# Attention and token mixer on one core: a written order of steps replaced by another

## The chip, the core and the metric

The kernel runs on one core of a Trainium2 chip. The metric is the device time of one execution in microseconds (us), the median over runs. The engines are named as in the profile: PE is TensorE's products, PEld its weight loads, DVE is VectorE, ACT is ScalarE, POOL is GpSimd and SP is SyncE, which here only issues DMAs.

## The reference

There are 8 batches of 8 heads, 576 tokens and 64 values per head, and 32 packed queries p.

```python
def sm_attn(qq, kk, vv):
    s = scale * np.matmul(qq, kk.transpose(0, 1, 3, 2))
    a = np.exp(s - np.max(s, axis=-1, keepdims=True))
    a = a / (np.sum(a, axis=-1, keepdims=True) + 1e-09)
    return np.matmul(a, vv)

p_packed = sm_attn(p, k, v)
x = sm_attn(q, p_packed, p_packed)          # heads side by side: (8, 576, 512)
wq, wk = x @ w_q, x @ w_k                   # (512, 64) each
W_tok = scale * np.einsum('bsd,btd->bst', wq, wk)
mixed = np.einsum('bst,btd->bsd', W_tok, x)
out = np.maximum(mixed, 0.0) @ w_out        # (512, 512), float32
```

## The kernel before

The work is cut into steps with short names, and a string named `ORDER` (lines 13 to 57) lists them one after the other. A loop at the end of the kernel (lines 602 to 624) reads a step such as `AM.3.2@P` or `OT.2.0=2,3`: the name, the batch, mostly a part of the batch, after `@` the engine (A ScalarE, V VectorE, P GpSimd, S SyncE) and after `=` the banks of the accumulator memory (PSUM, 8 banks) that its result takes. Under `tc.manual_schedule()` each engine runs its own steps strictly in that order; across engines they wait by semaphores for data, and for a buffer or a bank to come free.

For one batch the steps are these. KT (a block transpose of k on VectorE, line 237, as are TE, PT and QV), S1 (scores of p and k, line 282), X1 (exponential, two halves, ScalarE, line 293), TE (transposes of the exponentials), PV (their product with v and a column of ones, line 315), RC and PP (one over the sum, and the packed values, lines 319 and 323), PT (their transpose, `ppT`). QK multiplies ppT with w_q and w_k (line 336), QKE copies it out and QD doubles a part of it on GpSimd. QV transposes q, S2 multiplies it with ppT (line 373; parts 0 and 1 are two tiles of 128 tokens each, 2 is the rest, 3 is four tiles at once), X2 is its exponential (line 378), RS and RR its sums and their reciprocals (lines 394 and 399), and AM the product `a` = exponential times reciprocal (line 405), on GpSimd or VectorE. AT transposes a on TensorE (lines 414 and 419), AE copies that out, WKQ makes wk and wq (lines 441 and 446) and WE copies them out. The token mixing is regrouped: GM is a^T wk (line 467), Y is that times the packed values (line 477), MX and MR are mixed's columns (lines 492 and 498), with the copies GE and YE between them. RL, RLF (quarter of a relu) and RLR are the relus (line 503 on ScalarE, 505 on VectorE), OT and OH the product with w_out (lines 540 and 580), and OE, OEF and OEH copy it out of the accumulator memory (lines 128 and 132), from which ST, STF and STH store it. OT.b.4 is the last ninth of the tokens of a pair of batches.

Loads (LD, lines 157 to 182) are issued on GpSimd's own queue, since they turn float32 into bf16 on the way. A GpSimd load has one of eight semaphores in turn, so it is issued only when the eighth before it has landed, and what stands behind it on GpSimd waits too. k, q and v have four buffers each, results for storing six (`o`), the exponentials and most others two or three. HOLD.v7 is a tiny DMA on SyncE's queue that waits for the last v, so that the stores queued behind it on that engine start only then.

WARM steps are products of zeros that go nowhere, in float32, in pieces of at most 512 columns (the number is in units of 128 columns); they fill stretches in which TensorE has to wait. They are on line 619.

```python
                n = 128 * int(f[1])
                wide = int(f[2]) if len(f) > 2 else 512
                while n > 0:
                    w = min(n, wide)
                    ...
                    nc.tensor.matmul(bank(int(bk), [w]), warm[:, 0:P], rhs, start=True, stop=True)
                    n -= w
```

## Time and profile before

| | |
|---|---|
| median of 3 runs | 104.53 us (104.41 to 104.62) |
| profiled execution, first to last instruction (span) | 102.8 us, granted clock 1.000 |
| profiled execution's own time | not given apart; the median of the runs is 1.73 us above the span |
| TensorE, VectorE, ScalarE, GpSimd busy | 92.7, 73.7, 65.0, 51.8 us |
| read and written in device memory | 30.15 MB and 9.44 MB |

The rows of a timeline show the start in us, the duration in us, the engine, the line, the operation, the tile written and the tile read with their shapes, and how many instructions were put together; in brackets stands how long the engine sat idle before it and whose work ended that. Groups show the sum of busy time in us, the mean duration of one in ns and, behind the bar, the idle time before them. Ends of TensorE's products are modelled, so two rows can overlap by some tenths.

### The profile page before, as it was taken

How to read it: one execution, taken by the hardware profiler on the slowest of the kernel's cores; microseconds unless marked ns; L12 is line 12 of the kernel's file. 1: busy time of each engine (PE TensorE's matmuls, PEld its weight loads, DVE VectorE, ACT ScalarE, POOL GpSimd, SP SyncE). 2: the span in 40 equal slices, each digit the busy share in tenths (PEclk: the TensorE clock that was granted, in tenths of full speed). 3: DMA queues.
4: the chain of work that ended last, by engine and by line, in shares of the span. 5: the costliest groups of instructions: out<-in, count | busy, mean ns of one | idle time of the engine just before them, and what ended most of it. 6: DMA issues, size and time to landing. Idle time of an engine off the chain costs nothing.

```text
span 102.8 us, 3593 instructions
## 1 busy us (share of the span) xinstructions
PE 92.7 (90%) x1536; PEld 54.6 (53%) x1536; DVE 73.7 (72%) x140; ACT 65.0 (63%) x111; POOL 51.8 (50%) x81
## 2 busy tenths in 40 slices
PE   5995999998698899999998899989999999999940
PEld 3894454555364733655546556643757664743420
DVE  4173366966979479898597979689999979339520
ACT  2320406168853767938986979897889897735540
POOL 5971866993029938925349574558615009100000
PEclk9999999999999999999999999999999999999999
DMA  0999999999999999999999999999999999986894
GB/s 9 249 230 207 213 210 213 207 209 213 205 211 207 212 211 210 213 205 212 211 212 207 211 213 204 217 211 203 255 262 409 411 410 408 418 345 264 335 364 160
DMA packets 13279, 25.13 MB, mean 244 GB/s; under 512 B 1040, under 2 KB 6416, under 8 KB 13008
## 3 DMA queue, kind: packets, MB, share of 16 engines
q0 software_dynamic: 9648, 17.04, 84.0%
q1 hardware_dynamic: 3056, 7.41, 19.0%
q10 hardware_dynamic: 560, 0.46, 1.7%
q8 instruction: 12, 0.20, 0.7%
q14 instruction: 3, 0.02, 0.1%
HBM read 30.15 MB, written 9.44 MB: 385 GB/s over the span
## 4 chain that ended last, share of the span: by engine, by line
PE 49%; DMA 21%; DVE 8%; POOL 7%; ACT 6%; issue 3%; SPq 1%; DVEq 0%; POOLq 0%; ACTq 0%
PE ps L540 26%; DMA q_sb<-in_q_dram 13%; DMA o<-in_moe_w_q_dram 8%; PE ps L373 4%; POOL a L405 4%; PE ps L315 3%; ACT e1T L293 3%; PE ps L419 3%; PE ps L446 3%; DVE rs L394 2%; PE ps L441 2%; PE ps L467 2%; PE ps L282 2%; ACT e L378 1%; DVE qT L237 1%
## 5 line engine op out<-in xcount | busy, mean ns | idle before, releaser
L540 PE MATMUL ps<-wout,relu 128*128 128x512 bf16 x124 | 30.6, 380 | 0.0
L405 POOL TENSOR_TENSOR a<-e,rr 128x256 bf16<-128x256 f32 (+2 forms) x18 | 19.5, 1099 | 17.9 <-DVE rr L399 7.0
L619 PE MATMUL ps<-o 128*128 128x128 f32 (+3 forms) x76 | 19.5, 401 | 1.2 <-DVE o L135 1.2
L540 PEld LDWEIGHTS <-relu 128*128 128x128 bf16 x124 | 10.7, 98 | 11.7 <-issue 1.1
L128 ACT ACTIVATE o<-ps 128x1024 f32<-128x1024 f32 (+2 forms) x13 | 11.3, 871 | 5.4 <-PE ps L540 5.2
L619 PEld LDWEIGHTS ps<-o 128*128 128x128 f32 x76 | 11.3, 209 | 5.2 <-issue 3.6
L503 ACT ACTIVATE relu<-ps 128x1024 bf16<-128x1024 f32 (+1 forms) x14 | 13.0, 968 | 1.1 <-PE ps L492 1.1
L293 ACT ACTIVATE e1T<-ps 128x576 bf16<-128x576 f32 x16 | 9.8, 656 | 5.8 <-PE ps L282 5.2
L378 ACT ACTIVATE e<-ps 128x256 f32<-128x256 f32 (+2 forms) x19 | 11.2, 623 | 2.7 <-PE ps L373 2.5
L394 DVE TENSOR_REDUCE rs<-e 128x16 f32<-128x512 f32 (+2 forms) x13 | 10.9, 840 | 2.3 <-ACT e L378 2.2
L237 DVE STREAM_TRANSPOSE kT<-k_sb 128x1152 uint32<-128x1152 uint32 (+1 forms) x9 | 11.1, 1230 | 1.9 <-DMA k_sb<-in_k_dram 1.9
L173 POOL DMA_DIRECT2D v_sb<-in_v_dram x16 | 10.0, 628 | 4.0 <-DMA v_sb<-in_v_dram 1.6
L237 DVE STREAM_TRANSPOSE qT<-q_sb 128x1152 uint32<-128x1152 uint32 (+1 forms) x10 | 11.0, 1108 | 0.1
L132 DVE COPY o<-ps 128x1024 f32<-128x1024 f32 (+2 forms) x7 | 6.8, 977 | 5.3 <-PE ps L540 2.7
L237 DVE STREAM_TRANSPOSE e<-e1T 128x288 uint32<-128x288 uint32 x16 | 7.4, 468 | 3.1 <-ACT e1T L293 2.7
L128 ACT ACTIVATE aT<-ps 128x128 bf16<-128x128 f32 (+2 forms) x11 | 5.0, 465 | 5.7 <-PE ps L419 3.3
L128 ACT ACTIVATE wkq<-ps 128x448 bf16<-128x448 f32 (+1 forms) x10 | 7.2, 730 | 1.8 <-PE ps L446 1.7
L315 PE MATMUL ps<-v_sb,e 64*64 64x192 bf16 x288 | 7.5, 245 | 0.8 <-DVE e L237 0.5
L315 PEld LDWEIGHTS <-e 64*64 64x64 bf16 x288 | 5.9, 107 | 2.6 <-DVE e L237 2.1
L373 PEld LDWEIGHTS <-qT 64*128 64x128 bf16 x320 | 5.4, 94 | 2.8 <-DVE qT L237 1.7
L373 PE MATMUL ps<-ppT,qT 64*128 64x64 bf16 x320 | 6.6, 190 | 0.2 <-DVE qT L237 0.2
L446 PE MATMUL ps<-aT,pqk 128*128 128x256 bf16 (+1 forms) x48 | 6.8, 246 | 0.0
(70 smaller groups left out, 130.3 us busy)
## 6 DMA issues: line engine op xcount, KB each, us to landing
v_sb<-in_v_dram POOLq DMA_DIRECT2D x16, 288.0 KB, 13.9
out_dram<-o SPq DMA_DIRECT2D x9, 512.0 KB, 9.3
k_sb<-in_k_dram POOLq DMA_DIRECT2D x7, 576.0 KB, 13.6
q_sb<-in_q_dram POOLq DMA_DIRECT2D x6, 576.0 KB, 13.6
out_dram<-o POOLq DMA_DIRECT2D x2, 1024.0 KB, 11.3
out_dram<-o SPq DMA_DIRECT2D x5, 256.0 KB, 2.5
q_sb<-in_q_dram POOLq DMA_DIRECT2D x4, 288.0 KB, 10.4
out_dram<-orem SPq DMA_DIRECT2D x3, 256.0 KB, 8.5
```

What stands on the lines that cost most here:

```text
L128: nc.scalar.activation(o, i, COPY)
L173: nc.gpsimd.dma_start(v_bufs[b % NL][halves(i), 0:7:2], src)
L237: nc.vector.transpose(o, i)
L293: nc.scalar.activation(e1T[:, x], T["s1", b][x].rearrange("a c m -> a m c"), EXP, scale=scale)
L315: nc.tensor.matmul(T["pv", b][halves(cc), i], lhsT, rhs, start=n == 0, stop=n == R - 1, skip_group_check=True)
L373: nc.tensor.matmul(ps[:, y, t - t0, i], lhsT, rhs, start=e == 0, stop=e == 1)
L378: nc.scalar.activation(e2[:, t0:t1].rearrange("a t (i y n) -> a y (t i) n", i=2, y=2), T["s2", b, c].rearrange("a y t i n -> a y (t i) n") ...
L394: nc.vector.tensor_reduce(rs[:, t0 * H:t1 * H], src, axis=AX, op=ADD)
L405: e.tensor_tensor(a2[:, t0:t1].rearrange("a t i (u l) -> a (t i u) l", l=L), e2v(b, c), T["rr", b][:, t0 * H:t1 * H].to_broadcast((P, (t1 ...
L503: nc.scalar.activation(o, i, RELU)
L540: nc.tensor.matmul(ps, lhsT, wout[:, j, :], start=j == 0, stop=j == NJ - 1)
L619: nc.tensor.matmul(bank(int(bk), [w]), warm[:, 0:P], rhs, start=True, stop=True)
```

## The change

Only the string `ORDER` is another one. It has two lines fewer, so that every later line of the kernel has a number smaller by 2. Up to the transposes of batch 0 (`AT.0.1`) each engine keeps its order, with other banks; from there on the steps of all batches stand in another order. Two fillers of three units are added (behind `AT.0.1` there are six runs where there were four), and others moved. Some steps go to another engine: the products AM.1.1, AM.3.2, AM.4.2, AM.6.2 and AM.7.0 from GpSimd to VectorE and AM.6.3 back, YE.0 and YE.3 to ScalarE, YE.2, YE.5 and YE.7 to VectorE, QKE.1, QKE.3 and QKE.5 to ScalarE and QKE.4 to VectorE, and some copies and relus. The load of v7 is issued behind the two halves of q7 (r7 and q7), where it stood ahead of them, and the three stores that GpSimd issues are moved behind all loads.

```diff
-S1.1=0,1,4,5 WE.0.1@A GM.0=6 X1.1.0@A TE.1.0@V GE.0@A WARM.2=7 Y.0=2,3 YE.0@V S1.2=0,1,6,7 MR.0=2,3 X1.1.1@A
-TE.1.1@V MX.0.0=4,5 X1.2.0@A LD.O PV.1.0=0,1 TE.2.0@V PV.1.1 X1.2.1@A TE.2.1@V RC.1@V LD.k3 PP.1.0@V PP.1.1@V
-PT.1@V MX.0.1=6,7 QV.1.2@V RLR.0@A QK.1=2 QKE.1@V RL.0.0@A WARM.3=3 S2.1.2=4,5 S2.1.0=0,1 RL.0.1@A X2.1.2@A
-RS.1.2@V RR.1.2@V S2.1.1=2,3 X2.1.0@A RS.1.0@V RR.1.0@V WARM.1=6 PV.2.0=6,7 PV.2.1 X2.1.1@A RS.1.1@V RC.2@V
...
-HOLD.v7 MR.3=0,1 RC.5@V PP.5.1@V OE.2.1@A MX.3.0=2,3 PP.5.0@V PT.5@V MX.3.1=6,7 RLR.3@A RL.3.0@A OT.3.4=0
...
-STF.6.3 YE.7@A ST.5.0 MR.7=6,7 RLR.7@A MX.7.0=4,5 RLF.7.0.1@A RLF.7.0.0@V MX.7.1=2,3 RLF.7.1.0@A OT.7.4=0
-OEF.7.4@A ST.7.4 RLF.7.1.1@V OT.7.1=6 OEF.7.1@V OT.7.0=7 STF.7.1 OT.7.2=1 OEF.7.0@A OH.7.0=0 STF.7.0 OEF.7.2@A
...
+AT.0.1=1 AE.0.1@A AE.0.0@V WKQ.0.0=6,7 WKQ.0.2 WE.0.0@A LD.q2 WKQ.0.1 KT.2.2@V S1.1=2,3,4,5 WE.0.1@A WARM.3=0
+X1.1.1@A TE.1.1@V LD.O GM.0=0 X1.1.0@A GE.0@A S1.2=6,7,4,5 Y.0=2,3 TE.1.0@V X1.2.1@A PV.1.0=0,1 PV.1.1 X1.2.0@A
+YE.0@A TE.2.0@V MX.0.1=4,5 RC.1@V WARM.3=6 WARM.2=6 PP.1.1@V MX.0.0=6,7 PP.1.0@V WARM.3=2 PT.1@V QK.1=0 RL.0.0@A
+QV.1.2@V TE.2.1@V S2.1.2=2,3 QKE.1@A S2.1.0=6,7 X2.1.2@A LD.k3 MR.0=0,1 RS.1.2@V X2.1.0@A WARM.1=2 S2.1.1=2,3
...
+RS.3.4@V RR.3.4@V RL.2.1@A RC.4@V OT.2.0=4,5 PP.4.1@V LD.v6 AM.3.2@V OT.2.1 AM.3.3@P QD.3@P PP.4.0@V AT.3.2=0
...
+WKQ.3.1 X2.4.2@A WE.3.2@A KT.5.2@V OT.2.2=0,1 RS.4.4@V S1.5=2,3,6,7 RR.4.4@V OT.2.3 AM.4.3@P LD.q6 X1.5.1@A
+MR.2=4,5 GM.3=6 QK.4=7 X1.5.0@A OE.2.1@A TE.5.1@V TE.5.0@V GE.3@A PV.5.0=2,3 Y.3=0,1 LD.k7 RLR.2@V AM.4.2@V QKE.4@V
...
+WE.7.0@A GM.7=2 GE.7@A OE.5.0@V ST.4.0 ST.2.1 OT.6.1 OE.6.0@A Y.7=4,5 YE.7@V OT.6.2=2,3 MX.7.1=0,1 MX.7.0=4,5
+ST.1.8@P ST.5.1 ST.5.0 MR.7=6,7 RLF.7.0.0@V OEF.6.2@A RLF.7.0.1@A OT.6.3 RLF.7.1.1@V STF.6.2 ST.6.0 RLF.7.1.0@A
+RLR.7@V OT.7.0=4 OT.7.1=5 OEF.7.1@A OEF.6.3@V OEF.7.0@V STF.6.3 OT.7.2=0 OT.7.4=1 OH.7.0=2 OEF.7.2@V OH.7.1=0
```

TensorE around the end of PV.1 and QK.1 (the rows of lines 492 and 490 are MX.0, 336 and 334 QK.1, 619 and 617 fillers, 373 is S2.1), before:

```order
L336 LDWEIGHTS ppT_1_250
L336 MATMUL ps_61<-wqk_63,ppT_1_250 64x128
L619 MATMUL ps_61<-o_1_86 128x384
L373 LDWEIGHTS qT_1_268
L373 MATMUL ps_61<-ppT_1_250,qT_1_268 128x64
```

and now:

```order
L490 LDWEIGHTS y_0_502
L490 MATMUL ps_61<-wkq_0_363,y_0_502 128x512
L617 MATMUL ps_61<-o_1_86 128x384
L617 MATMUL ps_61<-o_1_86 128x256
L490 LDWEIGHTS y_0_502
L490 MATMUL ps_61<-wkq_0_363,y_0_502 128x512
L490 LDWEIGHTS y_0_502
L490 MATMUL ps_61<-wkq_0_363,y_0_502 128x512
L617 MATMUL ps_61<-o_1_86 128x384
L334 LDWEIGHTS ppT_1_250
L334 MATMUL ps_61<-wqk_63,ppT_1_250 64x128
```

The filler of 384 columns has moved from behind QK.1 to ahead of it, and two more runs stand between the halves of MX.0.

ScalarE over the same stretch (e1T is X1, g GE, rem RLR, relu RL, e2 X2, y YE, pqk QKE), before:

```order
L293 ACTIVATE e1T_0_194<-ps_61 128x576
L128 ACTIVATE g_0_420<-ps_61 128x128
L293 ACTIVATE e1T_0_194<-ps_61 128x576 x3
L503 ACTIVATE rem_0_522<-ps_61 128x4x64
L503 ACTIVATE relu_0_534<-ps_61 128x1024 x2
L378 ACTIVATE e2_1_84<-ps_61 128x2x2x64
L378 ACTIVATE e2_1_84<-ps_61 128x2x4x64 x2
```

and now:

```order
L291 ACTIVATE e1T_0_194<-ps_61 128x576 x2
L126 ACTIVATE g_0_423<-ps_61 128x128
L291 ACTIVATE e1T_0_194<-ps_61 128x576 x2
L482 ACTIVATE y_0_502<-ps_61 128x256
L501 ACTIVATE relu_0_526<-ps_61 128x1024
L126 ACTIVATE pqk_1_264<-ps_61 128x2x128
L376 ACTIVATE e2_1_84<-ps_61 128x2x2x64
L376 ACTIVATE e2_1_84<-ps_61 128x2x4x64 x2
L501 ACTIVATE relu_0_526<-ps_61 128x1024
L501 ACTIVATE rem_0_629<-ps_61 128x4x64
```

YE.0 and QKE.1 have come to ScalarE, and RL.0.1 and RLR.0 have moved behind X2.1.

VectorE from batch 3's sums to the start of batch 5 (rs is RS, rr RR, rec RC, pp PP, qT QV, ppT PT, aT AE, kT KT, e1 TE), before:

```order
L394 TENSOR_REDUCE rs_0_283<-e2_1_84 128x40
L399 RECIPROCAL rr_1_286<-rs_0_283 128x40
L319 RECIPROCAL rec_1_240<-ps_61 128x2
L323 SCALAR_TENSOR_TENSOR pp_1_244<-ps_61,rec_1_240,mask_79 128x128 x2
L237 STREAM_TRANSPOSE ppT_1_250<-pp_1_244 128x128
L237 STREAM_TRANSPOSE qT_1_268<-q_sb0_73 128x2x2x288
L132 COPY aT0_80<-ps_61 128x2x512
L237 STREAM_TRANSPOSE kT_1_124<-k_sb1_70 128x2x2x288
L394 TENSOR_REDUCE rs_0_283<-e2_0_83 128x40
L399 RECIPROCAL rr_0_285<-rs_0_283 128x40
L237 STREAM_TRANSPOSE e1_1_197<-e1T_0_194 128x9x32 x2
L486 TENSOR_SCALAR y_0_429<-ps_61 128x256
```

and now:

```order
L392 TENSOR_REDUCE rs_0_283<-e2_1_84 128x40
L397 RECIPROCAL rr_1_286<-rs_0_283 128x40
L317 RECIPROCAL rec_1_240<-ps_61 128x2
L321 SCALAR_TENSOR_TENSOR pp_1_244<-ps_61,rec_1_240,mask_79 128x128
L403 TENSOR_TENSOR a2_0_328<-e2_1_84,rr_1_286 128x256
L321 SCALAR_TENSOR_TENSOR pp_1_244<-ps_61,rec_1_240,mask_79 128x128
L235 STREAM_TRANSPOSE qT_1_268<-q_sb0_73 128x2x2x288
L235 STREAM_TRANSPOSE ppT_1_250<-pp_1_244 128x128
L130 COPY aT0_80<-ps_61 128x2x512
L235 STREAM_TRANSPOSE kT_1_124<-k_sb1_70 128x2x2x288
L392 TENSOR_REDUCE rs_0_283<-e2_0_83 128x40
L397 RECIPROCAL rr_0_285<-rs_0_283 128x40
```

AM.3.2 (the row of line 403) has come in between the two halves of PP.4, and PT.4 stands behind QV.4; behind these rows VectorE does TE.5, RLR.2, AM.4.2 and QKE.4 ahead of RC.5, where before it did TE.5 and YE.3.

## The prediction

> **What bounds the kernel now.** I read the totals first, then busy time by stage, then TensorE's own rows in each stage with the waits in brackets, and last what VectorE, ScalarE and GpSimd do at those waits. The totals:

> ```profile
> span 102.8 us, 3593 instructions
> ...
> PE 92.7 (90%) x1536; PEld 54.6 (53%) x1536; DVE 73.7 (72%) x140; ACT 65.0 (63%) x111; POOL 51.8 (50%) x81
> ...
> HBM read 30.15 MB, written 9.44 MB: 385 GB/s over the span
> ```

> TensorE is busy for 90% of the span, and no other engine comes near. The stages (start:end, length, then busy us and count for TensorE, its weight loads, VectorE, ScalarE and GpSimd, then granted clock, DMA share, GB/s):

> ```profile
> 36.00:51.10 15.10, 14.91 (x250) 7.45 (x245) 12.13 (x20) 11.39 (x18) 8.36 (x12) 1.00 1.15 210
> 51.10:68.60 17.50, 16.18 (x354) 9.64 (x352) 14.54 (x26) 15.26 (x24) 11.33 (x14) 1.00 1.14 210
> 68.60:79.20 10.60, 10.60 (x198) 6.35 (x202) 10.36 (x16) 8.93 (x15) 5.54 (x6) 1.00 1.13 274
> 79.20:99.00 19.80, 19.67 (x243) 10.73 (x242) 13.34 (x26) 13.58 (x26) 2.86 (x4) 1.00 0.93 369
> ```

> From 36.0 to 99.0 us TensorE idles 0.19 + 1.32 + 0.00 + 0.13 = 1.64 us. That, and what stands before 36.0, is all that another order can win, since the products after that point are the same ones. The only stage with something to lose from is 51.1 to 68.6, where VectorE and ScalarE are at 83% and 87%. The clock is 1.00 throughout. The last stage has a second limit: the DMA share is 0.93, so a faster TensorE there gains at most 0.07 x 19.8 = 1.4 us before the stores bound it.

> **The change, part by part.** No work is added but fillers; steps change place and engine. The queues of waiting work on VectorE, ScalarE and GpSimd decide, so I walk TensorE through the new order with durations of before.

> *The front (first difference at 22 us).* ScalarE and TensorE in before:

> ```profile
> 24.58 1.19 ACT L293 ACTIVATE e1T<-ps 128x576 bf16<-128x576 f32 x2 [0.27 <-PE ps L282]
> 25.66 0.39 ACT L503 ACTIVATE rem<-ps 128x256 bf16<-128x256 f32 x1
> 25.92 1.96 ACT L503 ACTIVATE relu<-ps 128x1024 bf16<-128x1024 f32 x2
> 29.28 1.36 ACT L378 ACTIVATE e<-ps 128x256 f32<-128x256 f32 x3 [1.40 <-PE ps L373]
> ```
> ```profile
> 27.51 0.41 PE L336 MATMUL ps<-wqk,ppT 64*64 64x128 bf16 x8 [0.97 <-DVE ppT L237]
> 27.85 0.91 PE L619 MATMUL ps<-o 128*128 128x384 f32 x2
> 28.94 0.78 PE L373 MATMUL ps<-ppT,qT 64*128 64x64 bf16 x40 [0.18 <-DVE qT L237]
> ```
> ```profile
> 31.24 1.32 PE L619 MATMUL ps<-o 128*128 128x512 f32 x4
> 32.44 0.40 PE L419 MATMUL ps<-idb,a 128*128 128x128 bf16 x4
> ```

> The filler of 640 columns took from 31.24 to 32.44, 0.24 us per 128 columns. Two more runs of 384 columns are 6 x 0.24 = 1.44 us of TensorE. They are not all lost: they stand where QK.1 waited 0.97 us at 27.51. YE.0 goes from VectorE to ScalarE, behind X1.2's two exponentials, which end at 25.77; with 0.3 for itself MX.0.1 starts at about 26.05. Then come half an MX, 640 columns of filler, the other half, 384 columns: 26.05 + 0.3 + 1.2 + 0.3 + 0.7 = 28.6 for QK.1 (27.51 before). But the filler that stood behind QK.1 now stands ahead of it, so S2.1.2 follows at about 29.1 against 28.94. Between S2.1.0 and S2.1.1 the 128-column filler now writes S2.1.2's bank and so waits for X2.1.2, which has QKE.1 ahead of it on ScalarE: S2.1.1's exponential ends at about 31.4, not 29.28 + 1.36 = 30.64.

> ```profile
> 31.34 2.05 POOL L405 TENSOR_TENSOR a<-e,rr 128x512 bf16<-128x512 f32 x2 [0.22 <-DVE rr L399]
> ```
> ```profile
> L237 DVE STREAM_TRANSPOSE qT<-q_sb 128x1152 uint32<-128x1152 uint32 x6 | 8.1, 1350 | 0.1
> ```
> ```profile
> 34.97 0.78 PE L373 MATMUL ps<-ppT,qT 64*128 64x64 bf16 x40
> 35.68 0.47 PE L467 MATMUL ps<-wkq,a 128*128 128x64 bf16 x10
> 35.98 0.38 PE L540 MATMUL ps<-wout,relu 128*128 128x512 bf16 x1
> ```

> AM.1.1 was the second half of GpSimd's 2.05 us and ended at 33.39. On VectorE it is shorter, which gives back most of the 0.76: it ends at about 33.5. QV.2.2, of 1.35 us, is queued behind it and PT.2, so it ends at 35.1, S2.2.2 starts at 35.15 (34.97), and WE.1.1, now on VectorE behind QV.2.2, holds GM.1 to 35.9. The first output product starts at 36.3 instead of 35.98: **+0.3**. If a producer's end and its reader's start never overlap as they do in these rows, the same walk gives +1.2; if the fillers fall wholly into waits, 0. I take +0.3, since pairs such as the 1.19 and 1.96 above show overlap.

> *36 to 51 us.* 0.19 us of idle in 15.1 and neither VectorE (12.1) nor ScalarE (11.4) is short; PV.3 and PV.4 have output products ahead of them as cover. OE.0.1, RL.1.1 and KT.4.2 are ahead of TE.3 on VectorE, covered by OT.1.2 and OT.1.3. **-0.1** (0 to +0.4).

> *51 to 68.6 us.* The waits that can go:

> ```profile
> 54.90 0.62 PE L419 MATMUL ps<-idb,a 128*128 128x128 bf16 x8 [0.44 <-POOL a L405]
> ...
> 57.66 0.48 PE L282 MATMUL ps<-kT,pT 32*32 32x288 bf16 x32 [0.32 <-DVE kT L237]
> ...
> 60.27 0.91 PE L315 MATMUL ps<-v_sb,e 64*64 64x192 bf16 x36
> ...
> 68.58 0.61 PE L315 MATMUL ps<-v_sb,e 64*64 64x192 bf16 x20 [0.47 <-DVE e L237]
> ```

> AT.3.3 waited 0.44 for GpSimd, S1.5 0.32 for KT.5.2. With AM.3.2 on VectorE, AT.3.2 runs first, and OT.2.2 now stands ahead of S1.5; both waits go (-0.76). What is late next is OT.2.0: its second input half hangs on RL.2.1, which stands on ScalarE behind X2.3.3 and RL.2.0 (RL of 1024 columns is about 1 us, from the 1.96 pair): +0.4. Together **-0.35**. Then PV.5: in before it started 60.27 - 57.66 = 2.61 after S1.5, with no wait, under OT.2.2, GM.3, OT.2.3 and Y.3. Now OT.2.2 (1.0) stands ahead of S1.5, and QK.4 (0.41) and MR.2 come in: about 2.1 of cover for the same chain of two exponentials (1.19) and two transposes, so a wait of 0.5, and 0.1 for AM.4.2 and RLR.2, which VectorE now does ahead of RC.5: **+0.6**. Cover restored by QK.5 ahead of PV.6 takes up to 0.4 of the 0.47, and MX.4.0 then waits for YE.4, behind OE.3.0 on ScalarE, +0.5: **+0.1**.

> *The products a = e x rr.* Where GpSimd's stood beside VectorE's own:

> ```profile
> L405 DVE TENSOR_TENSOR a<-e,rr x1: 1225/1225/1225, 76.7 to 76.7; 128x1024 bf16<-128x1024 f32 x1
> L405 POOL TENSOR_TENSOR a<-e,rr x1: 1577/1577/1577, 76.8 to 76.8; 128x256 bf16<-128x256 f32 x1
> ```
> ```profile
> L405 POOL TENSOR_TENSOR a<-e,rr 128x256 bf16<-128x256 f32 x8 | 5.8, 731 | 4.5 <-DVE rr L399 4.5
> ```

> 1225 ns for 1024 columns is 0.31 per 256, so VectorE gets 2 x 0.61 + 3 x 0.31 = 2.15 us for the five it takes over and gives back 1.23 with AM.6.3: small against its 73.7. But GpSimd's product took 1577 ns where that of VectorE ran, against a mean of 731: 0.85 longer. In the walk I let such a stretch fall into slack, bounds 0 and 0.85 each; the rival below prices it. [...]

> *68.6 to 79.2 us.* No idle now, VectorE busy 10.36 of 10.60. WE.5.2 is moved behind both of X1.7's exponentials on ScalarE, and GM.5 waits for it; AE.5.3 still comes before WKQ.5. One wait of a fraction of an exponential: **+0.2** (0 to +0.8).

> *The end.*

> ```profile
> 93.82 0.60 PE L492 MATMUL ps<-wkq,y 64*128 64x512 bf16 x4
> 94.47 1.04 PE L540 MATMUL ps<-wout,rem 128*128 128x512 bf16 x4
> 95.34 2.75 PE L540 MATMUL ps<-wout,relu 128*128 128x512 bf16 x12
> 97.93 1.04 PE L580 MATMUL ps<-wout,relu 128*128 128x384 bf16 x8
> ```

> OT.7.4, which needs no output of the last four relus, covered them at 94.47. Now only OT.6.3, as long, stands there, and VectorE has RLF.7.0.0, ScalarE OEF.6.2, ahead of the relus: +0.1. AM.7.0 goes to VectorE behind OEF.5.4, +0.1 at AT.7.0. **+0.2**. The stores of batch 7 come closer together, but as much follows TensorE's end as now: 3.8 us.

> Sum: 0.3 - 0.1 - 0.35 + 0.6 + 0.1 + 0.2 + 0.2 = +0.95. The profiled execution has 102.8 us from first to last instruction; the median of the runs is 104.53, 1.73 more, which I keep: 103.75 + 1.73 = 105.48, so **105.5 us**. A measurement of this kernel can tell about 0.2% (0.2 us) from no change.

> **Rivals.**

> *It is faster, 103.6.* The waits of 0.44, 0.32 and 0.47 us go and none of those that I add comes, because the transposes and relus overlap their readers more than I allow; the front still costs 0.3: 104.53 - 1.23 + 0.3 = 103.6. For: these are all real waits, and QK.1's 0.97 shows the front had room for fillers. Against: VectorE and ScalarE are at 83% and 87% there. It decides if PV.5 starts within 2.2 us of S1.5. The 1.4 us of the stores caps it at 103.1. Chance 0.27.

> *Slower by more, 107.2.* Two of GpSimd's products (AM.1.0 beside AM.1.1, AM.3.3 beside AM.3.2) are stretched by 0.85 each and lie on the path of AT.1.0 and AT.3.3: 105.5 + 1.7. [...] Chance 0.18.

> *The parts cancel, 104.5*, chance 0.08. *The change doesn't do what it says*: GpSimd's transfers do block it in before,

> ```profile
> 46.60 0.71 POOL L176 DMA_DIRECT2D k_sb<-in_k_dram  x1 [2.09 <-DMA q_sb<-in_q_dram]
> ...
> 52.93 2.48 POOL L405 TENSOR_TENSOR a<-e,rr 128x1024 bf16<-128x1024 f32 x2 [2.32 <-DVE rec L319]
> ```

> 2.09 us for a load to land, but the product behind it then sat for VectorE another 2.32 us. So knowing of the block gains nothing here; this feeds the forecast and has no chance of its own.

> **The numbers.** Forecast 0.47 (its own range by the bounds above 104.75 to 106.4), faster 0.27, much slower 0.18, cancelled 0.08. Faster by over 0.2%: 0.27; within: 0.08; slower: 0.47 + 0.18 = 0.65. The range reaches to the faster case's middle and near the slow one's: 103.5 to 107.0, with about 0.08 left out below and 0.12 above.

> **What would show it.** Right: first L540 product at about 36.3, PV.5 with a wait of about 0.5 for e of L237, no wait for GpSimd at AT.3.3, about 1.4 us more of filler on TensorE before 36, TensorE's end near 100. Wrong: that end before 98.7, or a first output product after 37, or GpSimd's products of 128x512 well over 1 us with TensorE behind them.

## The result and the profile after

The changed kernel takes 110.77 us (median of 5 runs, 110.37 to 111.6) against 104.53 us before (5 runs, 104.19 to 104.97): a ratio of 1.0601, 95% interval 1.0555 to 1.0647. Forecast were 105.5 us and a range of 103.5 to 107.0. The sign was right and the size was not: 6.2 us instead of 1.0. An execution more than 1.5% above the fastest of its kernel is left out of the ratios; that is one of `b_am32v`'s four (107.16 us) and no other.

The profiled execution took 111.6 us, the longest of the five, with a span of 109.7. Its page, by the rows that answer to those of before (the last row is the chain of work that ended last; below it the same row of before):

```profile
span 109.7 us, 3579 instructions
...
PE 96.5 (88%) x1525; PEld 57.0 (52%) x1540; DVE 76.6 (70%) x144; ACT 66.6 (61%) x111; POOL 49.9 (45%) x77
...
PEclk9999999999999999997599999999999999999998
DMA  2999999999999999999999989999892966999990
GB/s 22 228 227 208 213 216 210 202 215 204 215 208 212 210 205 213 207 213 212 206 213 211 212 149 149 210 207 209 182 388 94 396 264 264 411 403 394 390 356 13
...
PE 29%; DVE 23%; DMA 20%; issue 9%; POOL 8%; ACT 5%; SPq 1%; DVEq 0%; POOLq 0%; ACTq 0%
```
```profile
PE 49%; DMA 21%; DVE 8%; POOL 7%; ACT 6%; issue 3%; SPq 1%; DVEq 0%; POOLq 0%; ACTq 0%
```

Four things are new. The clock, full throughout before, falls in slices 18 and 19 of 40 (counted from 0, 2.74 us each: 49 to 55 us). "issue", time in which an engine waits for nothing that the profile shows, has 9% of the chain instead of 3%, and VectorE 23% instead of 8%. And the transfers have holes: at slices 30, 32 and 33 (82 to 93 us), where the stores should run, and, smaller, at 23 and 24 (63 to 68 us), where loads are queued on GpSimd behind AM.4.3. That second one I could not find on the path: PV.7 waits for VectorE (0.56 us, AE.6.2) and not for v7, the last load that it needs.

The front came out as forecast. TensorE's own rows around the first difference and at the first output product:

```profile
28.64 0.41 PE L334 MATMUL ps<-wqk,ppT 64*64 64x128 bf16 x8
29.22 0.54 PE L371 MATMUL ps<-ppT,qT 64*128 64x64 bf16 x24 [0.16 <-DVE qT L235]
...
35.08 0.78 PE L371 MATMUL ps<-ppT,qT 64*128 64x64 bf16 x40
35.79 0.47 PE L465 MATMUL ps<-wkq,a 128*128 128x64 bf16 x10
36.09 0.81 PE L538 MATMUL ps<-wout,relu 128*128 128x512 bf16 x2
```

QK.1 at 28.64 (forecast 28.6), S2.1.2 at 29.22 (29.1), S2.2.2 at 35.08 (35.15), the first output product at 36.09 against 35.98: +0.1 (forecast +0.3). The two more fillers cost next to nothing. Then, at 49.4 us, in the middle of the 40 products of S2.3 (the parts 2 and 3), first in before and then now:

```profile
48.62 1.01 PE L373 MATMUL ps<-ppT,qT 64*128 64x64 bf16 x40
```
```profile
48.71 0.69 PE L371 MATMUL ps<-ppT,qT 64*128 64x64 bf16 x34
50.86 0.31 PE L371 MATMUL ps<-ppT,qT 64*128 64x64 bf16 x6 [1.46 <-issue]
51.10 0.32 PE L475 MATMUL ps<-pp,g 64*64 64x128 bf16 x4
51.76 1.49 PE L538 MATMUL ps<-wout,relu 128*128 128x512 bf16 x3 [0.33 <-issue]
```

TensorE stands for 1.46 us between the 34th and the 35th of these products, both of part 3, which read the same tiles and write the same two banks, and the trace names nothing that releases it. The windows behind that stop (columns as in the prediction; the clock is the third number from the right):

```profile
50.00:51.00 1.00, 0.14 (x6) 0.15 (x6) 0.00 (x0) 0.00 (x0) 0.59 (x1) 0.97 1.11 210
51.00:54.20 3.20, 2.87 (x21) 0.77 (x22) 2.55 (x4) 1.40 (x2) 0.00 (x0) 0.50 1.12 209
54.20:56.00 1.80, 1.67 (x41) 0.96 (x40) 0.87 (x4) 1.80 (x3) 1.53 (x1) 0.96 1.23 214
```

For 3.2 us behind the stop the granted clock is 0.50, and three products of w_out that took 0.81 us in another run (the row at 49.88 further down) take 1.49. What came ahead of the fall in this trace is a gap of 1.46 us, among short products.

Further on, VectorE and GpSimd make the products a = e x rr of batch 3 (VectorE first, GpSimd second):

```profile
55.21 0.17 DVE L317 RECIPROCAL rec<-ps 128x2 f32<-128x2 f32 x1 [0.90 <-PE ps L313]
...
55.68 0.97 DVE L403 TENSOR_TENSOR a<-e,rr 128x256 bf16<-128x256 f32 x1
56.58 0.34 DVE L321 SCALAR_TENSOR_TENSOR pp<-ps,rec,mask 128x128 bf16<-128x128 f32 x1
56.84 1.36 DVE L235 STREAM_TRANSPOSE qT<-q_sb 128x1152 uint32<-128x1152 uint32 x1
58.13 0.26 DVE L235 STREAM_TRANSPOSE ppT<-pp 128x128 uint32<-128x128 uint32 x1
```
```profile
54.47 1.91 POOL L403 TENSOR_TENSOR a<-e,rr 128x1024 bf16<-128x1024 f32 x1 [3.87 <-DVE rr L397]
```

AM.3.2 took 0.97 us on VectorE, not 0.31. It ended at 56.65, just behind GpSimd's product (56.38), which took 1.91, as the four of that shape in before do with none of VectorE's beside them (1908 ns on average). All five products on VectorE, as groups, take 5.9 us, where the prediction had 2.15:

```profile
L403 DVE TENSOR_TENSOR a<-e,rr 128x256 bf16<-128x256 f32 x3 | 4.1, 1369 | 0.0
L403 DVE TENSOR_TENSOR a<-e,rr 128x512 bf16<-128x512 f32 x2 | 1.8, 904 | 0.0
```

The shortest, 0.68 us for 512 columns, is AM.1.1, which has no such product of GpSimd beside it (GpSimd's ends at 32.66, this one starts at 32.82). And at the end, SyncE's queue of stores and the windows (columns as above):

```profile
79.45 0.60 SPq L572 DMA_DIRECT2D touch<-v_sb  x1
83.21 0.63 SPq L561 DMA_DIRECT2D out_dram<-o  x1
```
```profile
80.00:84.00 4.00, 3.95 (x64) 2.59 (x50) 3.97 (x7) 3.74 (x6) 2.34 (x2) 1.00 0.59 234
84.00:88.00 4.00, 3.38 (x79) 2.33 (x79) 3.68 (x9) 2.48 (x4) 0.00 (x0) 1.00 0.90 350
88.00:92.00 4.00, 3.95 (x65) 2.13 (x65) 3.41 (x8) 3.54 (x9) 1.76 (x3) 1.00 0.57 214
92.00:96.00 4.00, 3.76 (x38) 2.29 (x37) 1.91 (x5) 2.58 (x4) 1.17 (x2) 1.00 1.02 402
```

The first store behind HOLD.v7 is ST.4.1, whose data is not there until 83.2; finished results of batches 2 and 3 are queued behind it. The same happens at 88 to 92 with ST.5.4. From 92 us on the transfers are full until about 107, 2.5 us behind TensorE's last product.

### The profile page after: what moved, and what is told of

Read it like the earlier page. It is cut to its first block, busy times and chain, and to the rows that moved or that the text cites. A ratio compares the mean times of both kernels' runs of the same rounds, so it can differ in the third digit from the quotient of the medians.

```text
span 109.7 us, 3579 instructions
## 1 busy us (share of the span) xinstructions
PE 96.5 (88%) x1525; PEld 57.0 (52%) x1540; DVE 76.6 (70%) x144; ACT 66.6 (61%) x111; POOL 49.9 (45%) x77
## 3 DMA queue, kind: packets, MB, share of 16 engines
HBM read 30.15 MB, written 9.44 MB: 361 GB/s over the span
## 4 chain that ended last, share of the span: by engine, by line
PE 29%; DVE 23%; DMA 20%; issue 9%; POOL 8%; ACT 5%; SPq 1%; DVEq 0%; POOLq 0%; ACTq 0%
PE ps L538 13%; DMA q_sb<-in_q_dram 13%; DMA o<-in_moe_w_q_dram 7%; DVE rs L392 6%; DVE a L403 5%; PE ps L313 4%; DVE qT L235 3%; PE ps L490 3%; DVE kT L235 2%; POOL v_sb L171 2%; PE ps L371 2%; ACT e L376 2%; DVE e L235 2%; DVE rr L397 2%; ACT e1T L291 2%
## 5 line engine op out<-in xcount | busy, mean ns | idle before, releaser
L403 POOL TENSOR_TENSOR a<-e,rr 128x256 bf16<-128x256 f32 (+2 forms) x14 | 16.6, 1199 | 32.6 <-DVE rr L397 26.9
L538 PE MATMUL ps<-wout,relu 128*128 128x512 bf16 x112 | 29.8, 387 | 1.1 <-issue 0.5
L617 PE MATMUL ps<-o 128*128 128x128 f32 (+3 forms) x80 | 22.0, 423 | 1.4 <-DVE o L133 1.2
L501 ACT ACTIVATE relu<-ps 128x1024 bf16<-128x1024 f32 (+1 forms) x15 | 13.9, 965 | 4.7 <-PE ps L490 4.4
L617 PEld LDWEIGHTS ps<-o 128*128 128x128 f32 x80 | 12.9, 224 | 6.5 <-issue 4.3
L126 ACT ACTIVATE o<-ps 128x1024 f32<-128x1024 f32 (+2 forms) x14 | 13.0, 927 | 3.7 <-PE ps L538 3.3
L313 PE MATMUL ps<-v_sb,e 64*64 64x192 bf16 x288 | 8.2, 247 | 1.4 <-DVE aT L130 0.6
L126 ACT ACTIVATE aT<-ps 128x128 bf16<-128x128 f32 (+2 forms) x11 | 5.5, 502 | 5.1 <-PE ps L412 2.2
L126 ACT ACTIVATE wkq<-ps 128x448 bf16<-128x448 f32 (+1 forms) x8 | 5.9, 734 | 1.7 <-PE ps L439 1.4
L439 PE MATMUL ps<-pqk,aT 128*128 128x64 bf16 x80 | 6.0, 194 | 0.4 <-ACT aT L126 0.2
```

Of the source, the lines that this page charges most:

```text
L126: nc.scalar.activation(o, i, COPY)
L313: nc.tensor.matmul(T["pv", b][halves(cc), i], lhsT, rhs, start=n == 0, stop=n == R - 1, skip_group_check=True)
L403: e.tensor_tensor(a2[:, t0:t1].rearrange("a t i (u l) -> a (t i u) l", l=L), e2v(b, c), T["rr", b][:, t0 * H:t1 * H].to_broadcast((P, (t1 ...
L501: nc.scalar.activation(o, i, RELU)
L538: nc.tensor.matmul(ps, lhsT, wout[:, j, :], start=j == 0, stop=j == NJ - 1)
```

## The experiments

Three causes were on the table: the stop and the clock behind it; the products on VectorE; the stores. To find out what the stop is, look at one row of the queues on the changed kernel's page (before has the same twelve packets):

```profile
q8 instruction: 12, 0.20, 0.6%
```

Twelve packets make 0.20 MB, 16 KB each, over the whole run: instructions arrive in blocks. In the trace of the changed kernel the fifth of them runs from 48.37 to 49.30 us, and the stop begins at 49.40. Theory I is that TensorE stands there for its next block of instructions; theory Q, that it waits for data and the trace doesn't name it. TensorE has 1525 + 1540 = 3065 instructions on the page above and 1536 + 1536 = 3072 in before, and no other engine more than 144, so these blocks are taken to be TensorE's: about 256 instructions each, an estimate (3072 / 12 = 256 and 3065 / 12 = 255). The trace of the changed kernel fits that: from this stop to a smaller one at 72.65, PV.6, which also comes behind a packet, the third after this one (70.78 to 71.74), TensorE's rows count 377 products and 383 weight loads, 760 / 3 = 253 to a packet.

**The same order, other places in the instruction stream** (`a_pad100`, and `b_pad100` as its control on the kernel before; `a_pad32` and `b_pad32` with the first of these lines alone):

```diff
-WARM.8=4
+PAD.32=4
-WARM.6=6 QK.0=0
+PAD.25=6 QK.0=0
-WARM.4=6 S2.0.2=6,7
+PAD.18=6 S2.0.2=6,7
-WARM.6=1 AT.0.2=0
+PAD.25=1 AT.0.2=0
...
+            elif f[0] == "PAD":
+                wb = warm.bitcast(bf16)
+                for _ in range(int(f[1])):
+                    nc.tensor.matmul(bank(int(bk), [P]), wb[:, 0:P], wb[:, P:2 * P], start=True, stop=True)
```

> The changed kernel with four float32 fillers of the first half (WARM.8, .6, .4, .6) replaced by 100 pairs of a weight load and a bf16 product of 128 columns, about as long, so that every later instruction of TensorE stands some 172 to 193 places further back in its stream. Order and engines of all steps are unchanged. Theory I (instruction supply: TensorE's instructions come in blocks of 256, and the stop of 1.46 us at 49.4 is the wait for a block that was asked for too late because the products before it are dense): the blocks now begin at other products, no stop over 0.3 us with the releaser 'issue' in 45 to 60 us, granted clock 0.998 to 1.000, time 107.0 to 108.5. Theory Q (the stop is a wait for data or a bank that comes with the new order and that the trace does not name): the stop stays at S2.3.3 and the time stays at 110 to 111.

> The changed kernel with only the filler WARM.8 replaced by 32 such pairs: some 56 to 62 places. Theory I: the block that began within S2.3.3 now begins about 60 instructions earlier, at S2.3's first products, where OT.1.0 and QK.3 give more time, so the stop there shrinks from 1.46 to below 0.5; but other blocks now begin at 25 and 69 us behind dense products, with stops of 0.4 to 1.3 there. Time 107.5 to 110. Theory Q: stop of 1.4 at S2.3.3 as before, 110 to 111.

> The kernel before with the same four fillers replaced by 100 pairs: control for the pairs themselves. Theory I: by the distance of each block's first instruction from the slow products ahead of it no stop over 0.2 us; time within 0.5 of before, 104.0 to 105.0. Theory Q: the same, since no order changes.

> The kernel before with only WARM.8 replaced by 32 pairs. Theory I: blocks of TensorE's instructions now begin behind dense products at about 26, 61 and 67 us, with stops marked 'issue' of some 0.4 to 1 us each, so that the kernel before becomes slower with no step moved: 105.0 to 107.0. Theory Q: no order changes, so 104.2 to 104.9.

Measured: `a_pad100` 108.52 us (ratio to before 1.0398, 1.037 to 1.0427), `a_pad32` 108.81 (1.0416, 1.0394 to 1.0438), `b_pad100` 104.89 (1.0043, 1.0025 to 1.0061), `b_pad32` 105.21 (1.0071, 1.0049 to 1.0093). TensorE in `a_pad100`:

```profile
48.76 0.78 PE L371 MATMUL ps<-ppT,qT 64*128 64x64 bf16 x40
49.47 0.25 PE L475 MATMUL ps<-pp,g 64*64 64x128 bf16 x4
49.88 0.81 PE L538 MATMUL ps<-wout,relu 128*128 128x512 bf16 x3 [0.16 <-issue]
...
55.08 0.23 PE L412 MATMUL ps<-idb,a 128*128 128x64 bf16 x2 [0.57 <-DVE a L403]
55.15 0.61 PE L417 MATMUL ps<-idb,a 128*128 128x128 bf16 x8
56.82 0.57 PE L371 MATMUL ps<-ppT,qT 64*128 64x64 bf16 x26 [1.05 <-DVE ppT L235]
```

All 40 products run through and the three products of w_out take 0.81. PV.4 starts at 51.15, the time of before (51.13), where it was 54.14. So the stop goes away with a change that moves no step. With what hangs on it, it was worth about 2.2 us (110.77 - 108.52). The same pairs make the kernel before slower by 0.6 us (104.89 - 104.32), and if they cost the changed kernel as much, the stop was worth 2.8; but there the first output product moves by only 0.04 us (36.09 to 36.13), where in the kernel before it moves by 0.28. The medians of before beside the two figures, 104.53 and 104.32, differ by 0.2 as well. A smaller stop of 0.42 us at PV.6 in the changed kernel (73.07) is gone too. For `b_pad32` I had expected stops of 0.4 to 1 us, and for `a_pad32` new ones at 25 and 69 us, and in neither do TensorE's products stop that long with the releaser "issue": the theory says what a stop is, but my rule for where one falls was not good enough to call it.

**Eight instructions** (`a_pad4`):

```diff
-WARM.22.128=0 S1.0=0,1,2,3
+WARM.22.128=0 PAD.4=0 S1.0=0,1,2,3
```

> The changed kernel with four pairs (8 instructions, 0.25 us) added ahead of S1.0, where TensorE waits for k anyway; nothing else. Theory I: the block begins 8 instructions (four products) earlier in the program, so the stop marked 'issue' comes after 30 of the 40 products of S2.3 instead of after 34, again 1.2 to 1.7 us long, and the time stays at 109.8 to 111.2. Theory Q: the stop, if it is a wait for data, stays after product 34.

```profile
48.66 0.63 PE L371 MATMUL ps<-ppT,qT 64*128 64x64 bf16 x30
50.79 0.32 PE L371 MATMUL ps<-ppT,qT 64*128 64x64 bf16 x10 [1.50 <-issue]
```

Four pairs more at 9 us, and the stop at 49 us comes four products earlier: 30 and 10 where it was 34 and 6. A wait for data can't do that; it is the place in the stream. 109.99 us (1.053, 1.0503 to 1.0556), 0.8 less than the changed kernel; the smaller stop at PV.6 is gone here too. The granted clock falls behind the stop as before, to 0.50 at 52 to 54 us. But one execution with a mean granted clock of 1.000, in which it can't have fallen so, took 109.79 us against 110.17 for the profiled one with 0.974: in this kernel the slow clock is worth no more than some 0.4.

**More time ahead of the block** (`a_split`):

```diff
-S2.3.2=4,5 S2.3.3=2,3 ... YE.2@V OT.1.1
+S2.3.2=4,5 OT.1.1 S2.3.3=2,3 ... YE.2@V
```

> The changed kernel with one step moved: OT.1.1 (four products of 512 columns, 0.74 us) between S2.3.2 and S2.3.3 instead of behind Y.2; the number of TensorE's instructions is the same. Theory I: TensorE reaches the block's first instruction 0.74 us later with the block asked for about when it was, so the stop shrinks from 1.46 to 0.4 to 0.8 us, the clock stays at full or nearly, time 108.3 to 109.7. Theory Q: the stop is as long or goes wholly, depending on which product waits; no change of 0.7 us in it is expected.

```profile
48.69 1.04 PE L538 MATMUL ps<-wout,relu 128*128 128x512 bf16 x4
49.66 0.51 PE L371 MATMUL ps<-ppT,qT 64*128 64x64 bf16 x22
50.57 0.32 PE L371 MATMUL ps<-ppT,qT 64*128 64x64 bf16 x10 [0.40 <-issue]
...
56.45 0.23 PE L412 MATMUL ps<-idb,a 128*128 128x64 bf16 x2 [0.87 <-DVE a L403]
```

The stop shrinks to 0.40 and the clock stays at 1.00 there, as theory I has it. The time doesn't follow: 111.25 us (1.0646, 1.0617 to 1.0675), a miss. S2.3's last products start only 0.3 us earlier (50.57 and 50.86), since OT.1.1 now stands in the way instead of the stop, and behind it X2.3, RS.3.4, RR.3.4 and AM.3.2 follow one another on ScalarE and VectorE; TensorE waits 0.87 for their end. In the changed kernel, too, the slow clock cost little by itself: PV.4 was 3.0 us late, S1.5 is 1.63 later than in `a_pad100` (60.91 and 59.28). VectorE stood 0.90 us for the late PV.4 (at 55.21), but AM.3.2 behind it then took 0.97 us instead of 2.01, since GpSimd's product was further on (begun 1.21 us earlier, in `a_pad100` 0.17). The stop's price is the delay of S2.3. By the profiled executions this kernel is 0.8 us shorter than the changed one (spans of 108.9 and 109.7), by the medians 0.5 longer. The profiled execution was the shortest of five (110.65 us, mean granted clock 0.993); the other four had 0.971 to 0.983, so the clock most likely fell in them; no trace shows where.

The link between the stop and the block is in the times of the transfers. The fifth packet begins at 48.37 us in the changed kernel, 48.40 in `a_pad4` and 48.16 in `a_split`, and TensorE goes on at 50.86, 50.79 and 50.57: 2.4 to 2.5 us later each time, whether it had stood 1.46, 1.50 or 0.40. What happens in the 1.4 to 1.6 us between the end of the transfer and that start no trace shows.

**The products back on GpSimd** (`a_amP`), **another order of stores** (`a_st`), **both** (`a_amP_st`), all on `a_pad100`:

```diff
-AM.3.2@V ... AM.4.3@P ... RLR.2@V AM.4.2@V ... AM.6.2@V
+AM.3.2@P ... AM.4.3@P AM.4.2@P ... RLR.2@V ... AM.6.2@P
```
```diff
-ST.0.8@P ... HOLD.v7 ... ST.4.1 ... ST.3.4 ... ST.3.1 ST.3.0 ... ST.5.4 ... ST.2.0 ... ST.4.0 ST.2.1 ... ST.1.8@P ST.5.1
+ST.0.8@P ST.1.8@P ... HOLD.v7 ST.2.0 ST.2.1 ST.3.4 ST.3.0 ST.3.1 ... ST.4.1 ST.4.0 ... ST.5.4 ... ST.5.1
```

> The padded changed kernel (108.52) with AM.3.2, AM.4.2 and AM.6.2 back on GpSimd. Theory P (the two engines exclude each other on such products: the one that starts second stands until the other is done, so AM.3.2 took 2.01 us on VectorE beside GpSimd's 1.91, against 0.61 on GpSimd alone): VectorE loses 5.1 us of such products, PT.4 comes 1.7 us earlier, the wait of 0.86 for ppT at S2.4 goes, AT.3.3 comes 0.4 later; S1.5 0.8 to 1.2 earlier, time 107.2 to 107.9. Theory W (these steps are no worse on VectorE, the loss at 55 to 60 us is of QV.4 ahead of PT.4): 108.3 to 108.8.

> The padded changed kernel with another order of stores only: on SyncE's queue ST.2.0, 2.1, 3.4, 3.0, 3.1 right behind HOLD.v7, then ST.4.1 and 4.0; on GpSimd's ST.1.8 right behind ST.0.8. Theory D (the end is set by the stores: some 4 us of transfer time are lost at 80 to 90 us because ST.4.1 and ST.5.4, not ready, stand ahead of ready ones): no gap at 80 to 90 us, end of the span 0.8 to 1.5 us earlier, 107.0 to 107.8. Theory E (TensorE's end at 102.2 and the last copies set it): at most 0.3 us, 108.2 to 108.6.

> Both edits together. Theories P and D: the sum of the two gains, 105.8 to 107.0. P alone: 107.2 to 107.9. D alone: as with the stores only.

Measured: 107.42 us (1.029, 1.0263 to 1.0318), 108.14 (1.0365, 1.033 to 1.0399) and 106.96 (1.0266, 1.0214 to 1.0318). The three products cost 1.1 us: theory P. TensorE in `a_amP` no longer waits at AT.3.2 (the first row) or at S2.4 (the last), but it waits for GpSimd at AT.3.3:

```profile
54.80 0.22 PE L412 MATMUL ps<-idb,a 128*128 128x64 bf16 x2
55.82 0.62 PE L417 MATMUL ps<-idb,a 128*128 128x128 bf16 x8 [0.80 <-POOL a L403]
56.38 0.78 PE L371 MATMUL ps<-ppT,qT 64*128 64x64 bf16 x40
```

The stores fill the holes, as the windows of `a_st` show:

```profile
80.00:84.00 4.00, 3.44 (x82) 2.54 (x80) 3.79 (x10) 2.62 (x5) 0.72 (x2) 1.00 1.02 407
84.00:88.00 4.00, 4.00 (x81) 2.38 (x77) 3.33 (x8) 3.80 (x8) 0.18 (x1) 1.00 1.02 399
88.00:92.00 4.00, 3.82 (x29) 1.80 (x29) 2.71 (x6) 3.24 (x4) 2.14 (x3) 1.00 0.95 369
92.00:96.00 4.00, 4.00 (x45) 2.20 (x43) 2.56 (x4) 1.75 (x3) 0.00 (x0) 1.00 0.38 153
```

But the medians differ by 0.4 us (108.52 and 108.14), not by 0.8 to 1.5, and the runs of the two overlap (108.11 to 108.83 and 108.01 to 108.65), so even that is not clear of the noise. The transfers are now down to 0.38 at 92 to 96 us, so the backlog is gone by then; OH.7.1 starts 0.2 us earlier (101.69 and 101.88). That is nearest to theory E.

**One product, in the kernel before** (`b_am32v`):

```diff
-AM.3.3@P AM.3.2@P ... PP.4.0@V PP.4.1@V
+AM.3.3@P ... PP.4.0@V AM.3.2@V PP.4.1@V
```

> The kernel before with one product moved: AM.3.2 from GpSimd to VectorE, between the halves of PP.4 as in the changed kernel, beside GpSimd's AM.3.3. Theory P: the 128x256 product takes 1.5 to 2.0 us on VectorE, PP.4, PT.4 and QV.4 behind it come 1.5 later, S2.4 starts 0.7 to 1.3 later, time 105.0 to 105.7. My price in the prediction (0.31 us for it): 104.2 to 104.7.

VectorE, GpSimd and TensorE in it:

```profile
52.88 2.01 DVE L405 TENSOR_TENSOR a<-e,rr 128x256 bf16<-128x256 f32 x1
```
```profile
52.71 1.91 POOL L405 TENSOR_TENSOR a<-e,rr 128x1024 bf16<-128x1024 f32 x1 [2.20 <-DVE rec L319]
```
```profile
55.56 0.41 PE L336 MATMUL ps<-wqk,ppT 64*64 64x128 bf16 x8 [1.67 <-DVE ppT L237]
```

105.42, 105.80 and 106.67 us against 104.45: a ratio of 1.0147 (1.009 to 1.0204). That is slower by about 1.5 us, more than theory P gave (105.0 to 105.7) and far more than my price did. The executions are far apart, with mean granted clocks of 0.992, 0.993 and 0.984; by the two with the higher clock the move costs 1.0 to 1.4 us. VectorE's product starts 0.17 us behind GpSimd's and takes 2.01 us; it ends 0.27 behind GpSimd's. GpSimd's takes 1.91, as those of before with none beside them (1908 ns on average). In the pair of before (76.67 and 76.79) VectorE started first, and GpSimd's ended 0.47 behind it. In both pairs the one that starts second is done only after the other.

**What is left** (`a_am_all`, on `a_amP_st`):

```diff
-AM.1.1@V ... AM.3.2@P OT.2.1 AM.3.3@P ... AT.3.2=0 ... AT.3.3=1 ... AM.6.2@P ... AM.6.3@P ... AM.7.0@V
+AM.1.1@P ... OT.2.1 AM.3.3@P AM.3.2@P ... AT.3.3=1 ... AT.3.2=0 ... AM.6.3@V ... AM.6.2@P ... AM.7.0@P
```

> The version with 100 pairs, three products back on GpSimd and the new order of stores (106.96), with all products a = e x rr now on the engines and in the order of before: AM.1.1 and AM.7.0 on GpSimd, AM.6.3 on VectorE, AM.3.3 ahead of AM.3.2 and AT.3.3 ahead of AT.3.2. If what is left (2.5 us over before, 2.0 over before with the pairs) comes from where these products stand: 105.0 to 106.0. If it comes from the order of the other steps (the forecast's own terms, about 1 us, and more): 106.5 to 107.2.

107.79 us (1.0327, 1.0294 to 1.0361): slower, outside both expectations. AM.1.1 on GpSimd is late in the new front:

```profile
34.73 0.40 PE L416 MATMUL ps<-idb,a 128*128 128x128 bf16 x4 [0.81 <-POOL a L402]
```

The first output product moves from 36.25 to 37.27 and the last one 1.0 later with it. So that one move to VectorE is worth 1 us to the new order. From the start of the first output product to that of OH.7.1 it takes 64.5 us here and in `a_amP_st`, and 62.6 in `b_pad100`: what is left on TensorE behind the front does not come from the engines of these products.

## Why the prediction was wrong

Start times of steps on TensorE, in us; the pairs shift the whole trace by 0.3 in the kernel before (and by 0.04 in the changed one), so the padded ones are compared with each other, by the time between steps:

| step | before | changed | forecast | `b_pad100` | `a_pad100` | `a_amP_st` |
|---|---|---|---|---|---|---|
| OT.0.0 | 35.98 | 36.09 | 36.3 | 36.26 | 36.13 | 36.25 |
| PV.4 | 51.13 | 54.14 | 51.3 | 51.42 | 51.15 | 51.27 |
| S1.5 | 57.66 | 60.91 | 57.5 | 57.94 | 59.28 | 58.61 |
| PV.5 | 60.27 | 63.33 | 60.7 | 60.55 | 61.70 | 61.02 |
| PV.7 | 79.22 | 83.79 | 80.0 | 79.49 | 81.55 | 81.15 |
| OH.7.1 | 98.58 | 104.11 | 99.5 | 98.84 | 101.88 | 100.76 |

*The front* (+0.3) was right, with its mechanism: fillers in a wait, AM.1.1 shorter on VectorE. Put back to GpSimd it costs 1.0.

*36 to 51 us* (-0.1): wrong by 3.0. Without the stop it is right: OT.0.0 to PV.4 takes 15.02 us in `a_pad100` and 15.16 in `b_pad100`, -0.14. The step that failed is the one that no row of before could price and that I did not list: that the same products in another order can be late because the instructions are. "The products after that point are the same ones" holds for the work, not for its delivery. This is 2.2 of the 5.3 us that were missed (2.8 if the pairs cost the changed kernel what they cost the kernel before).

*51 to 58 us* (-0.35): wrong. The waits at AT.3.3 and S1.5 did not simply go; in `a_pad100` AT.3.2, ahead of AT.3.3, waits 0.57 for VectorE and S2.4 1.05 for PT.4. The term that was mis-sized is AM.3.2 on VectorE: 0.31 in the sum, 0.97 and 2.01 in the traces. I had the rows of one pair side by side (VectorE's from 76.67, GpSimd's from 76.79) and read them one way only, as GpSimd's loss; in the three pairs shown the loss falls on whichever starts second, and here that was the engine with less slack. (The 0.85 itself was too small: the mean of 731 ns that it was taken from has the 1577 in it, and the other seven of that shape took 0.61.) The rival with this mechanism had the right cause (1.1 us in `a_amP`) on the wrong engine, and the right pair of steps in AM.3.2 and AM.3.3 only. With the products back, the wait at AT.3.3 that was to go is 0.8 us instead of 0.44.

*PV.5* (+0.6): not seen. S1.5 to PV.5 takes 2.42 in the changed kernel and in `a_pad100`, less than the 2.61 of before; the cover was enough.

*PV.5 to PV.7* (+0.1 and +0.2): too small by 0.9, by `a_amP_st`. The working called 51.1 to 68.6 "the only stage with something to lose from"; by its own rows VectorE was busy for 10.36 of 10.60 us in the next one.

*The end* (+0.2, and 3.8 us from TensorE's end to the end of the span): TensorE's share looks right (from PV.7 to OH.7.1 it takes 19.35 us in `b_pad100`, 19.61 in `a_amP_st`), but in the changed kernel 0.7 more, which goes with the products back on GpSimd. From the start of OH.7.1 to the end of the span it is 4.2 us in before (102.8 - 98.58), 5.6 in the changed kernel and 4.4 in `a_pad100`. I had noted that "the stores of batch 7 come closer together" and priced it at nothing; what that left out is that stores of batches 2 and 3 were queued behind ones of 4 and 5 that weren't ready. Another order of them, on `a_pad100`, was worth 0.4 at most; on the changed kernel itself, where the end is 1.4 us longer than in before, it was not tried.

*The change not doing what it says*: that GpSimd's blocked issues were off the path in before is not contradicted by any run, but no run tested it either.

In sum: the stop 2.2, the products 1.1, the stores 0.4 (within the noise), and 2.5 that remain between `a_amP_st` and before (106.96 - 104.45), in which the pairs themselves have somewhere from nothing to 0.6. On TensorE 1.9 us of it can be placed, from the table:

| stretch | forecast | `a_amP_st` against `b_pad100` |
|---|---|---|
| OT.0.0 to PV.4 | -0.1 | -0.14 |
| PV.4 to S1.5 | -0.35 | +0.82 |
| S1.5 to PV.5 | +0.6 | -0.20 |
| PV.5 to PV.7 | +0.3 | +1.19 |
| PV.7 to OH.7.1 | +0.2 | +0.26 |

The forecast had +0.65 for these rows together, and the traces have +1.93; the terms missed in both directions. PV.4 to S1.5 has the wait at AT.3.3. PV.5 to PV.7 is spread over small waits (0.63 at AT.4.2 is the largest); its cause stays open, and the one experiment on what remains (`a_am_all`) came out outside both expectations.

## What to carry to other kernels

TensorE here has a second input stream, its own instructions: 3065 of them, in twelve packets of 16 KB. When a trace shows a stop in the middle of a step with no releaser, look at the instruction queue's packets, and shift the stream by a few instructions: if the stop moves by as many, no data is at fault (here eight more instructions moved it from behind the 34th product to behind the 30th). An order worked out from waits for data alone has to be measured, since it doesn't know this stream (the stop was worth 2.2 us here). A product such as a = e x rr, moved to an idle-looking VectorE, is priced by what GpSimd runs beside it at that moment: 256 columns took 0.97 and 2.01 us on VectorE beside one of GpSimd's, and 512 columns took 0.68 with none beside them.
